# Retention attention and two MoE layers in one program: attention moved ahead of the first MoE, that MoE in two groups of 768 tokens, 224 places an expert

## The chip, the cores and the metric

The program runs on one core of a Trainium2 chip. The metric is the device time of one execution in microseconds (us). Engines are called PE (TensorE), DVE (VectorE), ACT (ScalarE), POOL (GpSimd) and SP (SyncE, which only issues transfers here).

## The reference, cut to what matters

```python
# attention: batch 2, 8 heads, 768 tokens, head size 64; one decay gamma per head
for t in range(S):
    state = gamma * state + k[:, :, t] (outer) v[:, :, t]
    y[:, :, t] = scale * (q[:, :, t] @ state)
# first MoE: one dense layer over 1536 tokens, 512 -> 2048 -> 512; w_in and w_out are float64
h = x @ w_in
sp = np.where(h > 20.0, h, np.log1p(np.exp(np.minimum(h, 20.0))))
g = h * np.tanh(sp)
x = g @ w_out
# second MoE: 8 experts, 512 -> 1024 -> 512; each token goes to its best expert
e_idx = np.argmax(x @ w_gate, axis=1)
for e in range(E):
    h = np.maximum(x[mask] @ w1[e], 0.0)
    out[mask] = gate_w[mask, None] * eom[mask, e, None] * (h @ w2[e])
```

gate_w is the softmax weight of the chosen expert and eom a sigmoid of a second small product. With the inputs used, the fullest expert gets 220 of the 1,536 tokens.

## The kernel before

**Attention.** A unit is a block of 128 tokens and a pair of heads; 12 blocks and 4 pairs give 48 units. In each, PE makes the scores of the two heads (`scores`, two float32 matmuls, L184 for the first 16 units with 64 rows of the array each, L187 from unit 16 on with 128 rows, where k of each head is padded with zeros), DVE multiplies them with the decay mask into `sm` (L189), and `values` multiplies them with v (L213), adds the query times the running state (L217) and makes the new state (L221). ACT and DVE take the result out of PSUM as two float32r parts, `xh` (L224) and `xl` (L231). POOL prepares `kh` and `qh` (L171, L176). The first 16 units run ahead of the first MoE; the other 32 are spread over the slices of its first two groups. For the first eight units PE also transposes k (`turn_k`).

**Decoding.** w_in and w_out come as float64. 32 words of 128x512 are brought to float32 by `decode`: one ACT conversion of the low word, four DVE steps (L260, L262, L266, L269) and one POOL addition (L271).

**First MoE.** Three groups of 512 tokens, 16 slices of 128 features each: 48 slices. For every slice, `splits` cuts the slice's part of w_in and of w_out into a high and a low float32r part (ACT copy L373, DVE subtraction L278); `up` makes 12 matmuls with 512 columns (L297) into one of two banks `hps`; `take_h`, `exp_h`, `mish_ln`, `mish_tanh` and `mish_split` turn the result into g in two parts (ACT L304, L309, L313, L317, L325; DVE L305, L318, L326), in batches of four slices so that ACT changes its function table seldom; `down`, five slices later (LAG), makes 3 matmuls with 512 columns for each of the group's four token blocks (L336 to L338) into four banks `acc`. The order of the steps inside a slice is written out by hand in `ORDER`; decoding runs beside the first group only, and the weights stay in SBUF for the later groups, which split them again.

**Router and second MoE.** The rows of a finished group go to DRAM, come back turned, and get their logits, their expert and their place (`logits_of`, `pick`, `rank`, `place`); `send` scatters them with indirect DMAs on POOL's queue to 256 places (CAP) for each expert. For the last group this happens between the last two slices' `down`, block by block; expert 0 gets its rows of the last group straight from PSUM by selection matmuls (`turn_base`, `select`, `part_rows`, `add_rows`), the others read theirs from DRAM (`load_rows`, `turn_x`). Each of 8 experts has 8 slices: `up2` makes 12 matmuls with CAP columns (L585), `down2` six with 512 (L601 to L603). `put` scatters the results. If any expert has more tokens than places, a general loop at the end computes the rest.

ACT follows the program order throughout; PE and DVE follow it in the stage ahead of the first MoE and in the last group's router, and elsewhere their order is left to the scheduler that builds the program.

Of the kernel before, what the change touches and what calls it, by code (L numbers as in the profile page):

```python
# [18 lines left out]
P = 128  # L19
# [4 lines left out]
E = 8  # L24
# [6 lines left out]
GB = 4  # L31
GT = GB * P
NG = NB // GB
CAP = 256
# [3 lines left out]
TBM = 2  # L38
TX0 = 6
LAG = 5  # L40
FILL = 1
FILL2 = 0
NFILL = 0
MV = 1
DS = [0, 0, 0, 1, 0, 0, 1, 1, 1, 1, 1, 1, 1, 1, 0, 1, 1]
EA = 0
HA = 0
HB = 0
TA = 0
TC = 1  # L50
KT = 8
SN = 3
EP = 0
RD = 2
S0 = 99
S1 = 15
WARM = 9
PLO0 = 1
LOVK = 0
PGL = (2,)  # L60
HIW = ()
HOW = ()
KP = 6
RL = 0
RT = 3
RG = 4
TB = [2, 2]
BE = [1, 2]
X1 = 0
X4 = 1  # L70
X5 = 1
X3 = 1
X2 = [[0, 1, 2], [3]]
# [12 lines left out]

# offsets (in float32 columns) in the constant array
# [5 lines left out]
C_ID = C_TOK + NB  # L93
# [8 lines left out]
def retention_moe_moe(ctx: ExitStack, tc: tile.TileContext, qkv, wraw, w12, wg, cst, pad, out):  # L102
# [12 lines left out]
    h_p = pool("h", NH)  # L115
    e_p = pool("e", NE)
    g_p = pool("g", NGB)
    u_p = pool("u", NU)
    s_p = pool("s", 2)
# [3 lines left out]
    acc, hps, mp, mt = [], [], [], []  # L123
# [11 lines left out]
    onesb = one.tile([P, P], BF16, name="onesb")  # L135
    mask = cs[:, C_MASK:C_MASK + H * P].rearrange("p (h t) -> p h t", h=H)
# [8 lines left out]
    tok = cs[:, C_TOK:C_TOK + NB]  # L145

    # ---------------- attention, one (block of 128 tokens, pair of heads) at a time
# [4 lines left out]
    def load_unit(n):  # L152
        blk, hp = units[n]
        if n < NU or n >= GB * KD:
            t = u_p.tile([P, 5, P], F32, name="u")
        else:
            t = (h_p if n % 2 else e_p).tile([P, GT], F32, name="h" if n % 2 else "e")
            t = t.rearrange("p (i t) -> p i t", i=4)
        w = 5 if n >= GB * KD else 4 if n >= KT else 3
        SP.dma_start(out=t[:, 0:w], in_=qkv[blk, hp, :, 0:w])  # L160
        unit_in[n] = t

    def prep_unit(n):
        blk, hp = units[n]
        t = unit_in[n]
        c = blk % CB
        kh = qh = None
        if c < CB - 1:
            kh = s_p.tile([P, 2, D], F32, name="kh")
            if n >= KT:  # L170
                G.tensor_tensor(  # L171
                    out=kh, in0=t[:, 4 if n >= GB * KD else 3].rearrange("p (j d) -> p j d", j=2),
                    in1=ktab[:, 2 * hp:2 * hp + 2].unsqueeze(2).to_broadcast([P, 2, D]), op=ALU.mult)
# [3 lines left out]
        unit_k[n] = (kh, qh)  # L177

    def scores(n, pst):
        blk, hp = units[n]  # L180
        t = unit_in[n]
        for j in range(2):
            if n < GB * KD:
                T.matmul(out=pst[:, j, 0:P], lhsT=t[j * D:(j + 1) * D, 1], rhs=t[j * D:(j + 1) * D, 0],  # L184
                         start=True, stop=True)
            else:
                T.matmul(out=pst[:, j, 0:P], lhsT=t[:, 1 + 2 * j], rhs=t[:, 0], start=True, stop=True)  # L187
        sm = s_p.tile([P, 2, P], F32, name="sm")
        V.tensor_tensor(out=sm, in0=pst[:, 0:2, 0:P], in1=mask[:, 2 * hp:2 * hp + 2], op=ALU.mult)  # L189
        return sm  # L190

    def turn_k(n, o):
        blk, hp = units[n]
        T.transpose(out=o, in_=unit_in[n][:, 1], identity=ident)
        for j in range(2):
            A.activation(out=unit_k[n][0][:, j], in_=o[:, j * D:(j + 1) * D], func=AF.Copy,
                         scale=ktab[:, 2 * hp + j:2 * hp + j + 1])

    def values(n, pst, sm):
        blk, hp = units[n]  # L200
        t = unit_in.pop(n)
        kh, qh = unit_k.pop(n)
        c = blk % CB
        g, o = blk // GB, (blk % GB) * P
        if n < GB * KD:
            ya, ua = pst[:, 0, P:2 * P], pst[:, 1, P:P + D]
        else:
            ya, ua = pst[:, 2], pst[:, 3, 0:D]
# [25 lines left out]
    # ---------------- weights: float64 words to float32, float32 to two float32r parts  # L234
# [14 lines left out]
    def decode(n):  # L249
        """The steps of a decoding, one vector instruction each."""  # L250
# [5 lines left out]
        if n < EA:  # L256
            A.activation(out=d.bitcast(F32), in_=hi.bitcast(F32), func=AF.Abs)
            A.activation(out=lo, in_=lo.bitcast(U32), func=AF.Copy, scale=2.0 ** -29)
        else:
            V.tensor_scalar(out=d, in0=hi, scalar1=0x7FFFFFFF, scalar2=None, op0=ALU.bitwise_and)  # L260
        yield
        (G if n < EP else V).tensor_scalar(out=d.bitcast(F32), in0=d.bitcast(F32), scalar1=2.0 ** -15, scalar2=None, op0=ALU.max)  # L262
        if n >= EA:
            A.activation(out=lo, in_=lo.bitcast(U32), func=AF.Copy, scale=2.0 ** -29)
        yield
        V.tensor_scalar(out=d, in0=d, scalar1=3, scalar2=0x3FFFFFF8, op0=ALU.logical_shift_left,  # L266
                        op1=ALU.bitwise_and)
        yield
        V.scalar_tensor_tensor(out=d, in0=hi, scalar=-0x40000000, in1=d, op0=ALU.bitwise_and,  # L269
                               op1=ALU.bitwise_or)  # L270
        G.tensor_tensor(out=d, in0=d, in1=lo, op=ALU.add)  # L271
        yield

    def split(src, name, engine=V, first=A):
        hi = t_p.tile([P, 512], F32R, name=name, bufs=6 if name == "wi" else NWO)
        lo = t_p.tile([P, 512], F32R, name=name, bufs=6 if name == "wi" else NWO)
# [6 lines left out]
    batches = [list(range(4 * i, 4 * i + 4)) for i in range((NS - sum(TB)) // 4)]  # L283
    for n in TB:
        batches.append(list(range(batches[-1][-1] + 1, batches[-1][-1] + 1 + n)))
# [3 lines left out]
    def up(i):  # L289
        g, f = divmod(i, NF)  # L290
        wh, wl = win.pop(i)
        xh, xl = xt[g, 0], xt[g, 1]
        o = hps[i % 2][:, :]
        n = 0
        for k in range(KD):
            for a, b in ((wh, xh), (wh, xl), (wl, xh)):
                T.matmul(out=o, lhsT=a[:, k * P:(k + 1) * P], rhs=b[:, k], start=(n == 0), stop=(n == 3 * KD - 1))  # L297
                n += 1

    def take_h(i):  # L300
        o = hps[i % 2][:, :]
        h = h_p.tile([P, GT], F32, name="h")
        e = e_p.tile([P, GT], F32, name="e")
        A.activation(out=h, in_=o, func=AF.Copy)  # L304
        V.tensor_scalar(out=e, in0=h, scalar1=20.0, scalar2=None, op0=ALU.min)  # L305
        hs[i], es[i] = h, e

    def exp_h(i):
        A.activation(out=es[i], in_=es[i], func=AF.Exp)  # L309

    def mish_ln(b):
        for i in b:
            A.activation(out=es[i], in_=es[i], func=AF.Ln, bias=1.0)  # L313

    def mish_tanh(b):
        for i in b:
            A.activation(out=es[i], in_=es[i], func=AF.Tanh)  # L317
            V.tensor_tensor(out=hs[i], in0=hs[i], in1=es.pop(i), op=ALU.mult)  # L318

    def mish_split(b):  # L320
        for i in b:
            h = hs.pop(i)
            gh = g_p.tile([P, GT], F32R, name="gh")
            gl = g_p.tile([P, GT], F32R, name="gl")
            A.activation(out=gh, in_=h, func=AF.Copy)  # L325
            (G if i < NF and i % 4 in PGL else V).tensor_tensor(out=gl, in0=h, in1=gh.bitcast(F32), op=ALU.subtract)  # L326
            gs[i] = gh, gl
# [19 lines left out]
    # ---------------- router, a block of 128 tokens at a time  # L347
# [13 lines left out]
    def blocks_of(r):  # L361
        return r.rearrange("p b c -> p (b c)")[:, 0:CAP * KD].rearrange("p (q j) -> p q j", j=P)

    def load_blocks(x, after=lambda i: None):
        """256 rows from DRAM, to be turned 32 by 32: row 32 q + r and feature 128 a + j to partition 32 a + r."""
        r = blocks_of(raw_p.tile([P, 2, RW], F32, name="raw"))
# [8 lines left out]
    def turn_rows(b, o, engine):  # L375
        r = rows[b // 2][:, b % 2]
        x = g_p.tile([P, KD * P], F32, name="gl")
# [17 lines left out]
    def logits_of(b0, n, o):  # L395
        """The logits of n blocks, each in a quarter of the columns of the tensor engine."""
# [19 lines left out]
    def tl(name, n, w, dtype=F32):  # L416
        return r_p.tile([P, n, w], dtype, name=f"{name}{n}", bufs=2 if n == 2 else 1)

    def pick(b0, n, o):
        """The experts of n blocks, from their logits."""  # L420
# [16 lines left out]
    def weigh(b0, n, o):  # L437
        """The exponentials of their weights."""
# [18 lines left out]
    def place(b0, n, o):  # L457
        """The places of the tokens among those of the experts."""
# [586 lines left out]
```

## Time and profile before

| what | value |
|---|---|
| median of 3 runs | 590.5 us (590.46 to 590.51) |
| the profiled execution, first to last instruction (its span) | 600.2 us |
| PE busy | 562.2 us, 94% |
| DVE busy | 418.5 us, 70% |
| ACT busy | 370.9 us, 62% |
| POOL busy | 155.4 us, 26% |

The runs are timed without the profiler, so the profiled span lies 9.7 us above their median. Busy time of PE counts matmuls whose ends are modelled and overlap, so 94% is no measure of how close PE is to its peak. Times inside the profile are us from the start of the span.

### The profile page before, as it was taken

To read this page: it belongs to the slowest core of one execution; us is meant where nothing else is said; L and a number is where in the kernel's file an instruction comes from. 1 tells how busy PE (TensorE), PEld (TensorE's weight loads), DVE (VectorE), ACT (ScalarE), POOL (GpSimd) and SP (SyncE) were. 2 spreads that over 40 slices of the span, in tenths; PEclk is the share of its full clock that TensorE was granted. 3 is DMA by queue.
4 is the path that set the end of the run, shared out by engine and by line. 5 is a ranking of instruction groups with operands and counts; after the bars stand their busy time and mean duration, and the time that the engine had idled before them with its cause. 6 is when DMAs were issued, how large, how long until landed. Compare 5 with 4: busy or idle time off the path is not lost.

```text
span 600.2 us, 9282 instructions
## 1 busy us (share of the span) xinstructions
PE 562.2 (94%) x3197; PEld 450.6 (75%) x3197; DVE 418.5 (70%) x858; ACT 370.9 (62%) x706; POOL 155.4 (26%) x163
## 2 busy tenths in 40 slices
PE   7997878798899999999999999999899999999992
PEld 4565556575667777777888788889699999999992
DVE  3569999999988384845536757548577687676650
ACT  3223665755767666665967969836466567566551
POOL 0357565485763131130000030023011011011011
PEclk9559889999899999999999999989999999999997
DMA  8625563535213374120016353605899778661001
GB/s 286 219 99 183 173 196 103 185 115 183 92 57 115 121 241 145 50 87 0 1 35 189 128 173 108 209 4 176 235 326 253 236 237 253 200 227 62 2 20 34
DMA packets 40388, 86.38 MB, mean 144 GB/s; under 512 B 6286, under 2 KB 19342, under 8 KB 40208
## 3 DMA queue, kind: packets, MB, share of 16 engines
q1 hardware_dynamic: 36432, 73.23, 39.5%
q10 hardware_dynamic: 1664, 6.19, 2.9%
q0 software_dynamic: 2240, 6.31, 2.8%
q8 instruction: 27, 0.44, 0.3%
q14 instruction: 25, 0.20, 0.1%
HBM read 76.21 MB, written 14.77 MB: 152 GB/s over the span
## 4 chain that ended last, share of the span: by engine, by line
PE 64%; DVE 23%; issue 4%; DMA 3%; ACT 2%; POOL 0%; ACTq 0%; SPq 0%; POOLq 0%; DVEq 0%
PE hps L297 15%; PE hps L585 12%; PE acc L336 6%; PE acc L338 6%; PE acc L337 5%; PE acc L601 4%; PE acc L602 4%; PE acc L603 4%; DVE fw L260 3%; DVE fw L266 3%; DVE fw L269 3%; DVE fw L262 3%; DVE e L305 2%; DVE wi L278 2%; DVE wo L278 2%
## 5 line engine op out<-in xcount | busy, mean ns | idle before, releaser
L297 PE MATMUL hps<-xh,wi 128*128 128x512 f32 x384 | 132.6, 407 | 2.0 <-DVE wi L278 2.0
L585 PEld LDWEIGHTS hps<-xh,wi 128*128 128x128 f32 x768 | 100.3, 191 | 7.3 <-ACT xh L574 1.7
L585 PE MATMUL hps<-xh,wi 128*128 128x256 f32 x768 | 102.6, 283 | 1.3 <-ACT xh L574 1.3
L278 DVE TENSOR_TENSOR wi<-fw,wi 128x512 fp32r<-128x512 f32 x108 | 77.9, 721 | 17.3 <-ACT wi L373 13.6
L297 PEld LDWEIGHTS hps<-xh,wi 128*128 128x128 f32 x384 | 74.5, 195 | 19.4 <-DVE wi L278 2.8
L278 DVE TENSOR_TENSOR wo<-fw,wo 128x512 fp32r<-128x512 f32 x109 | 78.1, 717 | 8.1 <-ACT wo L373 7.5
L297 PE MATMUL hps<-xl,wi 128*128 128x512 f32 x192 | 77.3, 403 | 0.0
L373 ACT CAST wo<-fw 128x512 fp32r<-128x512 f32 x109 | 68.0, 624 | 13.2 <-PE acc L602 12.8
L336 PE MATMUL acc<-wo,gh 128*128 128x512 f32 x180 | 73.2, 407 | 0.0
L373 ACT CAST wi<-fw 128x512 fp32r<-128x512 f32 x115 | 70.5, 614 | 2.0 <-issue 1.7
L337 PE MATMUL acc<-wo,gh 128*128 128x512 f32 x180 | 71.1, 395 | 0.0
L338 PE MATMUL acc<-wo,gl 128*128 128x512 f32 x180 | 69.8, 398 | 0.0
L271 POOL TENSOR_TENSOR fw<-fw,raw 128x512 int32<-128x512 int32 x32 | 52.5, 1648 | 37.1 <-DVE fw L269 18.3
L304 ACT ACTIVATE h<-hps 128x512 f32<-128x512 f32 x48 | 28.3, 589 | 50.1 <-PE hps L297 50.1
L614 POOL DMA_INDIRECT out_dram<-h,places x16 | 17.2, 1078 | 158.6 <-ACT h L613 136.4
L589 ACT ACTIVATE gh<-hps 128x256 fp32r<-128x256 f32 x64 | 24.6, 384 | 46.8 <-PE hps L585 46.3
L601 PE MATMUL acc<-wo,gh 128*128 128x512 f32 x128 | 50.5, 396 | 1.3 <-ACT gh L589 1.3
L602 PE MATMUL acc<-wo,gh 128*128 128x512 f32 x128 | 50.4, 395 | 0.0
L603 PE MATMUL acc<-wo,gh 128*128 128x512 f32 x128 | 49.7, 389 | 0.0
L318 DVE TENSOR_TENSOR h<-h,e 128x512 f32<-128x512 f32 x48 | 32.3, 717 | 21.8 <-ACT e L317 21.8
L590 DVE SCALAR_TENSOR_TENSOR gh<-hps,gh 128x256 fp32r<-128x256 f32 x64 | 26.8, 419 | 25.1 <-ACT gh L589 24.8
L297 PEld LDWEIGHTS hps<-xl,wi 128*128 128x128 f32 x192 | 37.5, 195 | 7.4 <-issue 0.2
(181 smaller groups left out, 944.3 us busy)
## 6 DMA issues: line engine op xcount, KB each, us to landing
fw<-in_w_dram SPq DMA_DIRECT2D x64, 512.0 KB, 4.1
raw<-in_wraw_dram SPq DMA_DIRECT2D x32, 512.0 KB, 3.7
u<-in_qkv_dram SPq DMA_DIRECT2D x32, 320.0 KB, 2.9
xs<-in_pad_dram ACTq DMA_DIRECT2D x8, 514.0 KB, 6.5
raw<-xs SPq DMA_DIRECT2D x28, 128.0 KB, 4.1
xall<-raw SPq DMA_DIRECT2D x4, 512.0 KB
raw<-xall SPq DMA_DIRECT2D x16, 128.0 KB, 3.2
e<-in_qkv_dram SPq DMA_DIRECT2D x4, 256.0 KB, 5.6
```

The source lines that it names most:

```text
L271: G.tensor_tensor(out=d, in0=d, in1=lo, op=ALU.add)
L278: engine.tensor_tensor(out=lo, in0=src, in1=hi.bitcast(F32), op=ALU.subtract)
L297: T.matmul(out=o, lhsT=a[:, k * P:(k + 1) * P], rhs=b[:, k], start=(n == 0), stop=(n == 3 * KD - 1))
L318: V.tensor_tensor(out=hs[i], in0=hs[i], in1=es.pop(i), op=ALU.mult)
L336: T.matmul(out=o, lhsT=gh[:, c], rhs=wh, start=(f == 0), stop=False)
L337: T.matmul(out=o, lhsT=gh[:, c], rhs=wl, start=False, stop=False)
L338: T.matmul(out=o, lhsT=gl[:, c], rhs=wh, start=False, stop=(f == NF - 1))
L373: (A.copy if engine is A else engine.tensor_copy)(out=to, in_=of)
L585: T.matmul(out=o, lhsT=a[:, k * P:(k + 1) * P], rhs=x[:, k, b:b + CAP], start=(n == 0), stop=(n == 3 * KD - 1))
L601: T.matmul(out=o, lhsT=g[:, c], rhs=wh, start=(f == 0), stop=False)
L602: T.matmul(out=o, lhsT=g[:, c], rhs=wl, start=False, stop=False)
L603: T.matmul(out=o, lhsT=g[:, l], rhs=wh, start=False, stop=(f == NF2 - 1))
```

## The change

Attention runs first: 42 of 48 units (NA) before the first MoE, the other six over its first three slices. All scores use 128 rows: one matmul with 256 columns per unit, k of both heads as weights, against q with the other head's half set to zero (`qz`, two ACT operations with a 0/1 column as scale). The 5-part layout of q, k and v and the transposes of k go. Every unit now loads four parts (256 KB).

The first MoE has two groups of 768 tokens: 32 iterations of two `up` halves with 384 columns each and a `down` over six blocks, three iterations later (LAG 3). The function is rewritten: tanh(softplus(h)) as -tanh(ln(sigmoid(-h))); the `min` on DVE and the Exp go, a Sigmoid from PSUM comes in. Batches are pairs of slices. Each decode step now has four DVE operations with no POOL in them; 34 of 128 steps (ND) run during attention and the others at a fixed rate of 6.8 an iteration. The copy of w_out's high part goes to DVE. Group 0's routing is one block of six; the last group's router handles six blocks, and sends the first four before the last `down` is over. CAP is 224, so `up2` has 224 columns and `down2` 112 columns of weights. PE, DVE and ACT follow the program order throughout.

```diff
-GB = 4
+GB = 6
 GT = GB * P
+GH = GT // 2
...
-CAP = 256
+CAP = 224
+CB2 = CAP // 2
...
-LAG = 5
+LAG = 3
+NA = 42
+WARM = 10
...
+ND = 34
...
+        qz = s_p.tile([P, 2, P], F32, name="qz", bufs=2)
+        for j in range(2):
+            A.activation(out=qz[:, j], in_=t[:, 0], func=AF.Copy, scale=halves[:, j:j + 1])
...
-        for j in range(2):
-            if n < GB * KD:
-                T.matmul(out=pst[:, j, 0:P], lhsT=t[j * D:(j + 1) * D, 1], rhs=t[j * D:(j + 1) * D, 0],
-                         start=True, stop=True)
-            else:
-                T.matmul(out=pst[:, j, 0:P], lhsT=t[:, 1 + 2 * j], rhs=t[:, 0], start=True, stop=True)
...
+        T.matmul(out=pst[0][:, 0:2 * P], lhsT=t[:, 1], rhs=unit_k[n][2].rearrange("p j t -> p (j t)"), start=True, stop=True)
...
-            V.tensor_scalar(out=d, in0=hi, scalar1=0x7FFFFFFF, scalar2=None, op0=ALU.bitwise_and)
...
-        G.tensor_tensor(out=d, in0=d, in1=lo, op=ALU.add)
...
+        V.tensor_scalar(out=d.bitcast(F32), in0=hi.bitcast(F32), scalar1=2.0 ** -112, scalar2=None, op0=ALU.mult)
+        A.activation(out=lo, in_=lo.bitcast(U32), func=AF.Copy, scale=2.0 ** -29)
         yield
...
+        V.tensor_scalar(out=d, in0=d, scalar1=3, scalar2=None, op0=ALU.logical_shift_left)
         yield
...
+        V.scalar_tensor_tensor(out=d, in0=hi, scalar=-0x80000000, in1=d, op0=ALU.bitwise_and,
+                               op1=ALU.bitwise_or)
         yield
...
+        V.tensor_tensor(out=d, in0=d, in1=lo, op=ALU.add)
         yield
...
+    def take_h(i, half):
+        if not half:
+            hs[i], es[i] = he(GT), he(GT)
+        c = slice(half * GH, half * GH + GH)
+        o = hps[half][:, 0:GH]
+        A.activation(out=hs[i][:, c], in_=o, func=AF.Copy)
+        A.activation(out=es[i][:, c], in_=o, func=AF.Sigmoid, scale=-1.0)
...
+            A.activation(out=es[i], in_=es[i], func=AF.Ln, bias=tiny)
+
+    def mish_tanh(i):
+        A.activation(out=es[i], in_=es[i], func=AF.Tanh, scale=-1.0)
+        V.tensor_tensor(out=hs[i], in0=hs[i], in1=es.pop(i), op=ALU.mult)
+
+    def mish_split(i, engine):
+        h, gh, gl = hs.pop(i), he(GT, F32R), he(GT, F32R)
+        copy(engine, gh, h)
+        V.tensor_tensor(out=gl, in0=h, in1=gh.bitcast(F32), op=ALU.subtract)
+        gs[i] = gh, gl
...
+            for n in range(NA + 1):
+                if n < NA:
+                    sm[n] = scores(n, spots[n % 3])
+                    prep_unit(n + 2)
+                steps_to(n - NA + ND)
+                if n >= NA - 1:
+                    split_in(n - NA + 1)
+                if n > 0:
+                    values(n - 1, spots[(n - 1) % 3], sm.pop(n - 1))
+                loads_to(n + 8)
+                raws_to(min(NR, max(0, n - 4) // 2))
...
+            s0 = ND + 4 * min(i, 3) + 34 * max(0, i - 3) // 5 + 2
+            mish_ln(b)
+            steps_to(s0)
+            late = range(NA + 2 * i, min(NA + 2 * i + 2, NU))
...
+            up(i, 0)
...
+            split_out(i + 2 - LAG)
+            take_h(i, 0)
+            if len(c) == 2:
+                mish_split(c[1], A)
+            if b:
+                mish_tanh(b[0])
+            split_in(i + 2)
+            steps_to(s0 + 2)
+            up(i, 1)
...
+            take_h(i, 1)
+            if len(b) == 2:
+                mish_tanh(b[1])
+            if b:
+                mish_split(b[0], A)
...
+            steps_to(s0 + 4)
+            if i >= LAG:
+                down(i - LAG, range(0, 3))
+                route(j)
+                down(i - LAG, range(3, GB))
...
+            if tb in (3, 5):
+                exps(n)
+                send(n, 2)
```

## Rows read from the trace of the kernel before

**Rows 1.** The page: busy time by engine, and the chain that ended last.
```profile
PE 562.2 (94%) x3197; PEld 450.6 (75%) x3197; DVE 418.5 (70%) x858; ACT 370.9 (62%) x706; POOL 155.4 (26%) x163
...
PE 64%; DVE 23%; issue 4%; DMA 3%; ACT 2%; POOL 0%; ACTq 0%; SPq 0%; POOLq 0%; DVEq 0%
```

**Rows 2.** Windows: stretch, length, busy time by engine (instructions), PE clock, DMA share, GB/s.
```profile
5.43:11.50 6.07, 5.89 (x58) 4.13 (x57) 2.36 (x8) 4.05 (x14) 0.35 (x1) 1.00 0.95 305
11.50:13.10 1.60, 0.06 (x3) 0.00 (x0) 0.81 (x4) 0.38 (x2) 0.38 (x2) 1.00 1.01 393
13.10:43.47 30.37, 30.36 (x200) 18.12 (x200) 16.79 (x51) 8.38 (x25) 13.09 (x26) 0.51 0.54 179
43.47:183.30 139.83, 118.68 (x604) 86.33 (x603) 136.75 (x230) 87.47 (x161) 87.76 (x71) 0.94 0.44 141
183.30:387.83 204.53, 204.53 (x1062) 162.41 (x1063) 125.18 (x281) 152.32 (x272) 26.25 (x37) 1.00 0.36 114
387.83:405.14 17.31, 16.88 (x118) 14.62 (x118) 8.13 (x38) 5.91 (x15) 5.11 (x4) 0.90 0.10 32
405.14:589.30 184.16, 181.57 (x1155) 163.77 (x1153) 127.86 (x248) 111.20 (x222) 20.41 (x19) 1.00 0.59 181
589.30:600.20 10.90, 0.22 (x1) 0.00 (x0) 0.00 (x0) 0.69 (x1) 1.83 (x2) 0.70 0.14 46
```

**Rows 3.** The chain in order of time: start, us, what.
```profile
248.88 1.01 PE mp L400 x32
...
304.62 2.72 PE hps L297 x12
310.06 2.72 PE hps L297 x12
...
414.63 6.04 DMA xs<-raw,idx
...
437.34 1.43 PE hps L585 x12
440.16 1.43 PE hps L585 x12
```

**Rows 4.** Timeline of PE around attention units: start, us, engine, line, operands, count.
```profile
28.34 0.80 PE L184 MATMUL sp<-h 64*128 64x128 f32 x4
...
30.73 0.80 PE L184 MATMUL sp<-e 64*128 64x128 f32 x4
...
41.74 2.08 PE L187 MATMUL mp<-u 128*128 128x128 f32 x8
...
192.56 0.60 PE L187 MATMUL mp<-u 128*128 128x128 f32 x4
...
193.09 0.44 PE L213 MATMUL mp<-sm,u 128*64 128x128 f32 x4
...
194.09 0.50 PE L336 MATMUL acc<-wo,gh 128*128 128x512 f32 x1
```

**Rows 5.** The chain inside the first group, DVE: start, us, what.
```profile
118.37 0.67 DVE fw L266 x2
...
120.24 2.41 DVE h L318 x4
```

**Rows 6.** Groups of ACT instructions by line, whole span: count, busy us, mean ns.
```profile
L304 ACT ACTIVATE h<-hps 128x512 f32<-128x512 f32 x48 | 28.3, 589 | 50.1 <-PE hps L297 50.1
...
L589 ACT ACTIVATE gh<-hps 128x256 fp32r<-128x256 f32 x64 | 24.6, 384 | 46.8 <-PE hps L585 46.3 <-issue 0.4
...
L313 ACT ACT_TABLE_LOAD x13 | 16.7, 1283 | 0.2
L317 ACT ACT_TABLE_LOAD x13 | 16.7, 1283 | 0.2
```

**Rows 7.** Timeline of the weight loads: 128 columns of weights, 16 columns streamed.
```profile
396.73 1.86 PEld L393 LDWEIGHTS hps<-wgs,gl 128*128 128x128 f32 x16
```

**Rows 8.** Waits from 44 to 175 us: us in total, times, longest.
```profile
ACT e L309 <- DVE e L305: 17.6, 11, 4.9
```

More of the change, by code (lines that the diff above doesn't have):

```diff
@@ L296, in up @@
             for a, b in ((wh, xh), (wh, xl), (wl, xh)):
-                T.matmul(out=o, lhsT=a[:, k * P:(k + 1) * P], rhs=b[:, k], start=(n == 0), stop=(n == 3 * KD - 1))
+                T.matmul(out=o, lhsT=a[:, k * P:(k + 1) * P], rhs=b[:, k, c], start=(n == 0), stop=(n == 3 * KD - 1))
                 n += 1
[L300 to L309, printed above, removed]
+        if half:
+            del win[i]
+    def take_h(i, half):
+        if not half:
+            hs[i], es[i] = he(GT), he(GT)
+        c = slice(half * GH, half * GH + GH)
+        o = hps[half][:, 0:GH]
+        A.activation(out=hs[i][:, c], in_=o, func=AF.Copy)
+        A.activation(out=es[i][:, c], in_=o, func=AF.Sigmoid, scale=-1.0)
     def mish_ln(b):
         for i in b:
[L313 to L327, printed above, removed]
+            A.activation(out=es[i], in_=es[i], func=AF.Ln, bias=tiny)
[7 more added lines that the diff above has]
+        gs[i] = gh, gl
     def down(i, tbs):
@@ new lines, in retention_moe_moe @@
+            for n in range(2):
+                prep_unit(n)
+            for n in range(WARM):
+                T.matmul(out=idle, lhsT=zeros[:, 0:P], rhs=zeros[:, 0:512], start=True, stop=True)
+            for n in range(NA + 1):
[9 more added lines that the diff above has]
+                raws_to(min(NR, max(0, n - 4) // 2))
@@ L818, in retention_moe_moe @@
         g = NG - 1
-        splits(NS + 2)
-        mish_tanh(batch_at[NS - 1])
-        mish_split(batch_at[NS - 1])
-        for n in range(NS - LAG, NS - TBM):
-            down(n, range(GB))
+        b0 = g * GB
+        mish_ln([NS - 1])
+        mish_tanh(NS - 1)
+        mish_split(NS - 1, A)
+        split_out(NS - 1)
+        down(NS - 3, range(GB))
         for m in range(NF - LAG, NF):
@@ new lines, in retention_moe_moe @@
+        add_rows(b0, 2, [2])
+        turn_rows(b0 + 5, hps[0], A)
+        logits(b0 + 4, lb[:, 0:2 * E])
+        logits(b0 + 5, lb[:, 2 * E:4 * E])
+        pick(b0 + 4, 2, lb)
+        add_rows(b0 + 2, 2, [0])
+        turn_base([3])
+        add_rows(b0, 2, [3])
+        add_rows(b0 + 2, 2, [1])
+        rank(b0 + 4, 2, rb)
+        place(b0 + 4, 2, rb)
+        add_rows(b0 + 2, 2, [2, 3])
+        select(b0 + 4, 0)
+        add_rows(b0 + 4, 1, range(KD))
+        select(b0 + 4, 1)
+        add_rows(b0 + 5, 1, range(KD), True)
@@ L920, in retention_moe_moe @@
                 turn_x(e + 1)
+            if m == NF2:
+                V.tensor_copy(out=meta[1], in_=meta[0][:, :, 0])
             if m == KP:
-                for b in (b0, b0 + 2):
-                    keep(b, A)
-                A.dma_start(out=xmore, in_=more)
+                for n in range(0, GB, 2):
+                    keep(b0 + n)
+                SP.dma_start(out=xmore, in_=more)
             if f == KP + 1 and e < E - 2:
```

542 lines of the change are left out of this document (184 added, 358 removed).

## The prediction

> **What bounds the kernel now.** I read the page first, then a table of windows cut at the stages, then the chain of waits, then timelines of PE. The page says PE 94% busy, and that PE holds 64% of the chain and DVE 23% [rows 1]. That average hides four stages [rows 2]:
>
> - 13.1 to 43.5 us: attention ahead of the first MoE, PE busy in every microsecond but at a granted clock of 0.51, its lower level of 1.2 GHz. A unit takes 2.39 us there [rows 4].
> - 43.5 to 183.3: group 0 of the first MoE. DVE is busy 136.75 of 139.83 us, PE 118.68, the clock averages 0.94. DVE is the bound.
> - 183.3 to 387.8: groups 1 and 2. PE is busy throughout at 1.00.
> - 405.1 to 589.3: the second MoE, PE again, 2.6 us idle.
>
> Between them lie 17.31 us of router, and 10.9 us at the end [rows 2].
>
> PE's prices at the full clock: twelve 512-column matmuls take 2.72 us, 0.2267 each, and a slice (up and down) 5.44 us; twelve 256-column ones take 1.43, 0.1192 each, and a slice of the second MoE 2.82 [rows 3]. From the two sizes a column costs 0.42 ns and a matmul 11.7 ns on top. An attention unit inside the first MoE takes 192.56 to 194.09, 1.53 us [rows 4].
>
> So the stretch from 43.5 to 387.8, 344.4 us, holds 48 ups and 46 downs (94 x 2.72 = 255.7) and 32 units (49.0), plus about 2 of logits: 307. The other 37 us are what DVE's bound in group 0 costs PE, in idle time and at the lower clock.
>
> **Stage by stage, after.**
>
> *Attention.* The first scores start at 5.43 now; two ACT operations on q come ahead, about 0.6, so 6.0. The new scores are two passes of 256 columns where L187 has four of 128: the same columns, so I keep the 0.53 us of L187 (192.56 to 193.09) and 1.53 for a unit, although units without a state need less. 42 x 1.53 = 64.3; with 0.5 for handing over, the first MoE starts at 70.8. This assumes the full clock. Other engines: DVE's three attention operations and one decode step make about 1.2 us a unit (decode pace below); 256 KB a unit and a 512 KB word every four units are 0.39 MB, 1.3 us at the 305 GB/s of 5.4 to 11.5 us [rows 2]. Both lie under 1.53, so PE sets the pace, but with little to spare.
>
> *First MoE on PE.* Columns are the same. 384 columns cost 0.0117 + 384 x 0.00042 = 0.173 us by the two sizes; an iteration is 24 x 0.173 + 18 x 0.2267 = 8.23 us, 32 of them 263.4, less the last two downs, which belong to the router: 255.2. Six late units cost 9.2. The logits of group 0, 1.01 us for four blocks [rows 3], come once for six: about 2.3.
>
> *First MoE on DVE.* Back to back in group 0, a single-source step takes 0.67/2 = 0.335 us and a two-source one 2.41/4 = 0.60 at 512 columns [rows 5]; 768 columns add half of 0.53, so 0.87. An iteration: 6.8 decode steps at a mean of 0.47 (3.2), w_in's subtraction 0.6, w_out's copy and subtraction 0.94, the multiplication and the low part 1.73: 6.5 us against PE's 8.23. Decode moves from POOL to DVE, but splits fall from 96 to 64 slices and `min` goes. If POOL's additions no longer slow DVE, group 0 becomes PE's. Against that stands before's own pace: 136.75/16 = 8.55 us a slice, with POOL's additions beside it. Taking from it the `min` (0.6) and attention (about 0.85) and adding the fourth step, the copy and the longer rows (1.0 + 0.34 + 0.53) gives 9.0, 0.8 over PE for 13 iterations: 10 us. Bounds 0 and 12; I take 5, nearer to the fast rows since POOL has nothing to do in those iterations. A wait is added: w_out's parts have six buffers, so an iteration's `split_out` waits until PE has ended the `down` before it; behind it on DVE stand that iteration's multiplication, low part and w_in's subtraction, which PE needs only an iteration later.
>
> *First MoE on ACT.* L304 takes 589 ns at 512 columns and L589 384 at 256 [rows 6], so 0.49 at 384 and 0.79 at 768. An iteration: four at 384 (1.95), three at 768 (2.4, 2.5 with the bias operand), w_in's copy 0.6, 1.7 conversions (1.1), one table load (1.28): 7.5 us in group 0, 6.3 after. That lies under 8.23, so nothing, but the cover is thin: ACT also issues the eight zero fills of the places in iterations 6 to 13, and what it needs beyond 0.7 us more in one of these PE waits for.
>
> *Router.* 17.31 us now, of which eight block-downs of 0.68 are 5.4. After: twelve of them, 8.2, the other 11.9, and 3.9 for two blocks more (bounds 2 and 6, by nothing but the selection matmuls and by the full proportion): 24.0. The last slice's chain (two takes 1.0, two table loads 2.6, Ln, Tanh and high part 2.4, DVE 1.7: 7.7 us) lies beside the two downs ahead of it, 8.2.
>
> *Second MoE.* At 224 columns the two sizes give 0.1058 us a matmul. But 128 columns of weights must be loaded for each, and where only 16 columns are streamed loads come 1.86 us less one 0.19 us record over 15, 0.111 apart [rows 7]: the load binds. Bounds 0.1058 and 0.1192 (no gain, 5.5 us more); I take 0.112, so 12 x 0.112 + 1.39 = 2.734 a slice, 64 of them 175.0, against 180.5 now. *The Trainium skill's page "TensorE: Matmul & The Clock Gate", section "LDWEIGHTS (loading the stationary operand)", speaks against the full saving too: a load takes its columns over 1.2 GHz, 107 ns for 128, an estimate of 171.5 us by itself; the trace, at 111, agrees within 4%.* The 3.7 us that 184.16 holds beyond 180.5 are a wait for expert 1's rows, behind four scatters whose last took 6.04 us to land [rows 3]. Two instead of four wait for the end now: I keep 1 us. Together 176.0. The end keeps its 10.9.
>
> **The sum.** 70.8 + 255.2 + 9.2 + 2.3 + 5 + 24.0 + 176.0 + 10.9 = 553.4 us of span, against 600.2: 46.8 less. The runs' median is 590.5, 9.7 below the profiled span; with the same difference, 543.7. I predict **544 us**.
>
> **Rivals.**
>
> *The attention stage stays at 1.2 GHz* (580 us). For: after 1.54 us without matmuls at 11.5 the clock fell, and from 13.1 to 43.5 it stayed low although PE never paused [rows 2]; a unit then took 2.39 [rows 4], so 42 x 0.86 = 36 us more, up to 42 with the wider scores at the pace of L187's eight passes at 41.74. Against: from 5.4 to 11.5 the same sparse units ran at 1.00, and PE now waits for no decode there. It decides if a transfer or ACT leaves PE empty that long once.
>
> *ACT paces the first MoE, and the kernel is slower* (619 us). Place: ACT's fixed order, in which Sigmoid and Tanh take turns within a pair of slices. If each change loads a table, that is four loads of 1.283 [rows 6] more per pair, 2.57 an iteration: 10.0 and 8.9 us, 584 in all. ACT's longest kind of wait for DVE in group 0, 17.6 us [rows 8] over 16 slices, 1.1 an iteration, on top gives 11.1 and 10.0: (2.9 + 1.8) x 16 = 75 us more. It turns slower once ACT needs 8.23 + 46.8/32 = 9.7 us an iteration. Against: 13 batches now load 13 tables for Ln and 13 for Tanh [rows 6], and the Exp between Tanh and Ln has no row of its own, so functions can share a table. *The Trainium skill's page "ScalarE: Activation LUTs", section "Table sets: the hidden batching unit", lists tanh in sigmoid's set, which speaks against this rival.*
>
> *DVE and ACT wait for each other in group 0* beyond my 5 us, both in program order: the 1.1 us of [rows 8] in each of 16 iterations is 18, so 557.
>
> *The 224 places bring nothing*: 549. *More tokens than 224 for an expert* would run the general loop; the fullest has 220.
>
> **How the numbers follow.** The forecast gets 0.55 (own range 530 to 566: no stalls, 0.1058 and units without state cheaper at one end; 12 us of stalls, no gain from 224 and a unit at 1.7 at the other). The low clock 0.25, part of it for only some of the stage, ACT's pacing 0.06, longer mutual waits 0.12; 0.02 for anything else. The range 528 to 586 takes in all but ACT's case and the edges. Two runs of this kernel can be told apart by about 0.2%. Faster 0.90, within 0.2% 0.02, slower 0.08: ACT's case and low clock together with waits.
>
> **What would show it.** PE clock 1.00 and some 1.5 us a unit until about 70 us; iterations of 8.2 us from the fourth on, DVE and ACT below 95% in them; two table loads a pair of slices; `up2` twelve in 1.34; first matmul of the second MoE near 366. The prediction is wrong if the clock row shows 0.5 after 15 us, if iterations of group 0 take over 9 us, or if ACT never idles.

## The result: 563.0 us against 590.5, and the profile after

The changed kernel takes 563.03 us (median of four executions, 561.92 to 563.54). The ratio to the kernel before is 0.9528, with a 95% interval of 0.9509 to 0.9548. The prediction was 544 us with a range of 528 to 586. One thing has to be known to read the times of this case: the kernel before takes about 590 us in some executions and about 600 in others, the version at the end of this text took 585.6 once in six, and ratios use the lower group.

The page of the changed kernel: busy time by engine, the granted clock in 40 slices (tenths), and the chain that ended last. The profiled execution took 561.92 us, its span is 560.2.

```profile
PE 539.9 (96%) x3311; PEld 451.9 (81%) x3311; DVE 369.2 (66%) x790; ACT 378.6 (68%) x722; POOL 75.7 (14%) x130
...
PEclk9999999999999999999999999999999999999997
...
PE 86%; DVE 4%; issue 4%; ACT 2%; DMA 1%; POOL 0%; POOLq 0%; DVEq 0%; ACTq 0%
```

DVE's 23% of the chain [rows 1] are down to 4%: PE now sets the pace nearly everywhere, at its full clock. The windows of the changed kernel, cut at its stages (columns as in [rows 2]):

```profile
5.59:10.02 4.43, 3.31 (x24) 1.93 (x23) 1.42 (x5) 2.63 (x9) 1.22 (x3) 1.00 1.06 383
10.02:70.66 60.64, 60.40 (x518) 33.27 (x518) 48.75 (x148) 41.98 (x129) 29.75 (x73) 1.00 0.85 285
70.66:71.99 1.33, 0.00 (x1) 0.03 (x1) 1.33 (x4) 0.82 (x3) 0.29 (x1) 1.00 0.35 139
71.99:342.50 270.51, 270.17 (x1429) 241.65 (x1430) 173.52 (x312) 208.82 (x331) 12.91 (x21) 1.00 0.33 102
342.50:345.81 3.31, 0.76 (x4) 0.32 (x3) 2.29 (x4) 2.30 (x4) 0.00 (x0) 1.00 0.00 0
345.81:373.61 27.80, 25.26 (x178) 20.29 (x179) 17.94 (x82) 10.65 (x25) 11.66 (x10) 1.00 0.37 134
373.61:549.68 176.07, 175.26 (x1154) 153.03 (x1153) 123.55 (x236) 108.52 (x221) 17.36 (x16) 1.00 0.62 178
549.68:560.20 10.52, 0.40 (x2) 0.00 (x0) 0.00 (x0) 0.69 (x1) 1.88 (x2) 0.64 0.16 48
```

From the second row to the seventh PE is idle for 0.24, 1.33, 0.34, 2.55, 2.54 and 0.81 us. Group 0, where PE lost 21 us in idle time alone [rows 2], has gone as a stage of its own. Against the terms of the sum:

| term | predicted, us | measured, us |
|---|---|---|
| first scores of the first MoE | 70.8 | 71.99 |
| from there to the last `down` ahead of the router, at 342.50 | 271.7 | 270.5 |
| router, to the first `up2` at 373.61 | 24.0 | 31.1 |
| second MoE | 176.0 | 176.1 |
| end | 10.9 | 10.5 |
| span | 553.4 | 560.2 |

The span was missed by 6.8 us, nearly all of it in the router. The other 11.4 us of the miss come from turning the span into a time: I took 9.7 us off, where the changed kernel's time lies 1.7 above its span (1.7 to 2.3 in every execution with both on record). The last 1.1 is the profiled execution's distance from the median.

Two places carry the gain. Against a profile of the kernel before with a span of 589.4 us (below), some 34 us are won up to the router and 8 in the second MoE, and 14 are lost in the router. An iteration of the first MoE in group 0, the chain in order of time (start, us, what):

```profile
102.69 4.18 PE hps L244 x24
...
111.00 4.18 PE hps L244 x24
...
119.31 0.71 PE hps L244 x4
```

8.31 us, 4.18 of them the two `up` halves, with no wait in the chain; 8.23 was predicted. And the second MoE, where a slice takes 2.73 us and twelve matmuls of `up2` 1.33, against 1.43 in [rows 3]:

```profile
432.49 1.33 PE hps L534 x12
...
435.22 1.33 PE hps L534 x12
```

The place that was missed is the end of the first MoE. The chain around the last slice's function and in the router:

```profile
335.24 0.85 ACT L262 ACTIVATE h<-h 128x768 f32<-128x768 f32 x1
```

```profile
338.09 1.28 ACT L259
...
340.34 1.28 ACT L262
...
342.52 0.97 DVE h L263
343.51 0.84 ACT h L312
344.37 0.96 DVE h L268
345.33 0.35 DVE wo L312
345.77 0.70 DVE wo L225
...
356.27 1.17 DVE at L404
...
365.33 1.20 DVE at L404
```

The first fence is the timeline: ACT is still at slice 30's Tanh while slice 31's `up` is over. Then Ln and Tanh of slice 31 load a table each, and DVE's split of w_out stands behind them; PE waits from 343.2 to 345.8. Later L404, an addition of 16 columns, twice takes over 1.1 us.

### The profile page after: what moved, and what is told of

Same layout as the page of the kernel before. It is cut to its first block, busy times and chain, and to the rows that moved or that the text cites. A ratio compares the mean times of both kernels' runs of the same rounds, so it can differ in the third digit from the quotient of the medians.

```text
span 560.2 us, 9429 instructions
## 1 busy us (share of the span) xinstructions
PE 539.9 (96%) x3311; PEld 451.9 (81%) x3311; DVE 369.2 (66%) x790; ACT 378.6 (68%) x722; POOL 75.7 (14%) x130
## 4 chain that ended last, share of the span: by engine, by line
PE 86%; DVE 4%; issue 4%; ACT 2%; DMA 1%; POOL 0%; POOLq 0%; DVEq 0%; ACTq 0%
PE hps L244 23%; PE hps L534 13%; PE acc L278 7%; PE acc L279 7%; PE acc L280 7%; PE acc L551 5%; PE acc L550 5%; PE acc L552 5%; PE sp L148 4%; PE sp L165 2%; PE sp L169 2%; PE sp L173 1%; DMA cs<-in_cst_dram 1%; DMA h<-in_qkv_dram 1%; PE acc L148 1%
## 5 line engine op out<-in xcount | busy, mean ns | idle before, releaser
L244 PE MATMUL hps<-xh,wi 128*128 128x384 f32 x512 | 137.8, 338 | 0.0
L534 PE MATMUL hps<-xh,wi 128*128 128x224 f32 x768 | 96.0, 274 | 0.8 <-DVE h L539 0.8
L244 PE MATMUL hps<-xl,wi 128*128 128x384 f32 x256 | 85.7, 335 | 0.0
L278 PE MATMUL acc<-wo,h 128*128 128x512 f32 x192 | 75.9, 395 | 2.6 <-DVE wo L312 2.6
L279 PE MATMUL acc<-wo,h 128*128 128x512 f32 x192 | 75.4, 393 | 0.2 <-DVE wo L225 0.2
L280 PE MATMUL acc<-wo,h 128*128 128x512 f32 x192 | 75.5, 393 | 0.0
L263 DVE TENSOR_TENSOR h<-h 128x768 f32<-128x768 f32 x32 | 30.7, 959 | 50.6 <-ACT h L262 47.0
L254 ACT ACTIVATE h<-hps 128x384 f32<-128x384 f32 x64 | 31.4, 491 | 48.2 <-PE hps L244 48.2
L551 PE MATMUL acc<-wo,h 128*112 128x512 f32 x128 | 50.7, 396 | 0.0
L550 PE MATMUL acc<-wo,h 128*112 128x512 f32 x128 | 50.6, 395 | 0.0
L552 PE MATMUL acc<-wo,h 128*112 128x512 f32 x128 | 50.3, 393 | 0.0
L312 ACT CAST wo<-fw 128x512 fp32r<-128x512 f32 x64 | 39.7, 621 | 11.1 <-PE acc L551 11.0
L142 ACT ACTIVATE qz<-h,cs 128x128 f32<-128x128 f32 x96 | 33.2, 394 | 19.6 <-PE sp L148 16.6
L278 PEld LDWEIGHTS acc<-wo,h 128*128 128x128 f32 x192 | 36.1, 188 | 10.3 <-ACT wo L312 3.0
L280 PEld LDWEIGHTS acc<-wo,h 128*128 128x128 f32 x192 | 36.0, 188 | 7.9 <-DVE h L268 0.3
```

The lines of the kernel that those rows point to most:

```text
L142: A.activation(out=qz[:, j], in_=t[:, 0], func=AF.Copy, scale=halves[:, j:j + 1])
L244: T.matmul(out=o, lhsT=a[:, k * P:(k + 1) * P], rhs=b[:, k, c], start=(n == 0), stop=(n == 3 * KD - 1))
L254: A.activation(out=hs[i][:, c], in_=o, func=AF.Copy)
L278: T.matmul(out=o, lhsT=gh[:, c], rhs=wh, start=(f == 0), stop=False)
L279: T.matmul(out=o, lhsT=gh[:, c], rhs=wl, start=False, stop=False)
L280: T.matmul(out=o, lhsT=gl[:, c], rhs=wh, start=False, stop=(f == NF - 1))
```

## Experiments: what the clock depends on

**The kernel before, profiled again.** No edit.

> The kernel before, unchanged, profiled anew. First theory: the profiled execution of before (span 600.2) was not like its timed ones; a profile of a 590.5 us execution has a span some 1.7 us below its own time, near 589, as in the changed kernel, and the 11 us lie in one stage: attention ahead of the first MoE, with a granted clock above the 0.51 of [rows 2]. Second theory: profiling costs this kernel 10 us, the span is 600 again and the clock is 0.51 again from 13 to 43 us.

Its four executions took 591.18, 601.88, 603.03 and 589.46 us; the profiled one is the first, with a span of 589.4. So the first theory holds: the profiled execution is one of the timed ones, and the profile of [rows 2], with a span of 600.2, was one of a 600 us execution. The same stretch in this profile, cut where the first MoE begins (windows; columns as above):

```profile
5.43:11.50 6.07, 5.95 (x60) 4.20 (x59) 3.34 (x12) 3.58 (x14) 0.86 (x2) 1.00 0.99 346
11.50:13.10 1.60, 1.60 (x19) 1.01 (x17) 0.86 (x4) 0.89 (x4) 0.04 (x1) 1.00 1.03 394
13.10:30.70 17.60, 16.94 (x186) 10.66 (x182) 15.32 (x43) 7.61 (x23) 13.61 (x24) 1.00 0.84 296
30.70:43.47 12.77, 10.50 (x58) 7.54 (x60) 10.92 (x25) 3.24 (x8) 7.58 (x9) 0.87 0.35 99
```

PE does not pause at 11.5, the clock stays at 1.00 where [rows 2] have 0.51, and the first MoE begins at 30.7 instead of 43.5. What made the pause in the 600 us execution is in its timeline, DVE and then PE:

```profile
12.29 0.43 DVE L260 TENSOR_SCALAR fw<-raw 128x512 int32<-128x512 int32 x1 [1.95 <-DMA raw<-in_wraw_dram]
```

```profile
13.11 0.38 PE L184 MATMUL sp<-h 64*128 64x128 f32 x2 [1.54 <-DVE xl L231]
```

DVE, in program order, waits 1.95 us for the first raw word; the `xl` that frees PE's PSUM stands behind it. A transfer that lands 2 us later thus cost that execution some 10 us, through the clock. This is not all that sets executions of the kernel before apart: the two of 601.88 and 603.03 us have mean clocks of 0.981 and 0.980, no lower than the 0.983 and 0.980 of the two short ones (the 600.2 us profile has 0.952), so they lost their time in another way, and no profile shows it.

**64-row scores in the changed kernel.** `qz` and its ACT operations go, `ua` moves to another part of its bank, and `sm` becomes two operations.

```diff
-        T.matmul(out=pst[0][:, 0:2 * P], lhsT=t[:, 1], rhs=unit_k[n][2]..., start=True, stop=True)
+        for j in range(2):
+            T.matmul(out=pst[j][:, 0:P], lhsT=t[j * D:(j + 1) * D, 1], rhs=t[j * D:(j + 1) * D, 0], start=True, stop=True)
```

> The changed kernel with the old form of scores: two matmuls with 64 rows each, no qz. First theory: PE keeps its full clock because nothing stops it in the first 15 us; the form of the scores does not matter for the clock. The clock row stays at 1.00, a unit drops from 1.63 to about 1.4 us (half the 2.39 at 1.2 GHz is 1.2; q, k, v and the words want 1.3), the time is 551 to 558. Second theory: scores with half the rows are too little work for the full clock; it falls to 0.5 within the stage, a unit takes 2.3, and the time is 585 to 600.

554.51 us (553.43 to 555.09), 8.5 less than the changed kernel, with the clock at 1.00 in every window of the stage: the first theory. (Against the 564.40 that a later set gave for the changed kernel it is 9.9 less.) One unit of the changed kernel and one of this kernel, timelines of PE:

```profile
30.16 0.70 PE L148 MATMUL sp<-qz,h 128*128 128x256 f32 x2
30.79 0.44 PE L165 MATMUL sp<-sm,h 128*64 128x128 f32 x4
31.16 0.44 PE L169 MATMUL sp<-qh,st 64*64 64x128 f32 x4
31.52 0.34 PE L173 MATMUL sp<-h,kh 128*64 128x64 f32 x4
31.79 0.70 PE L148 MATMUL sp<-qz,h 128*128 128x256 f32 x2
```

```profile
29.32 0.49 PE L146 MATMUL sp<-h 64*128 64x128 f32 x4
29.74 0.44 PE L164 MATMUL sp<-sm,h 128*64 128x128 f32 x4
...
30.74 0.49 PE L146 MATMUL sp<-h 64*128 64x128 f32 x4
```

1.63 and 1.42 us a unit; all of the difference lies in the scores, 0.63 against 0.42. So widening the scores to 128 rows made the kernel slower.

**A pause, with either form of scores.** ACT gets needless work ahead of unit 5 (six operations with 128 rows, eight with 64), so PE waits 2.88 and 2.85 us.

```diff
+                    if n == 3:
+                        for _ in range(6):
+                            A.activation(out=idle, in_=cs[:, C_MASK:C_MASK + 4 * P], func=AF.Copy)
                     prep_unit(n + 2)
```

> The changed kernel with six needless ACT operations of 128x512 ahead of unit 5's qz, so that PE stands still for some 2 us near 12 us, as before did at 11.5. First theory: units with 128-row scores are enough work to bring the clock back; it dips for a few us, and the time grows by 2 us of pause and 2 to 5 of low clock: 566 to 570. Second theory: after such a pause the clock stays at 1.2 GHz for all of the stage, as in before; 38 units take 0.8 us more each and the time is 593 to 603.

> The pause (eight ACT operations) and the 64-row scores together. First theory: the clock comes back only if the work after the pause is dense, and half-row scores are not; the clock row shows 0.5 from the pause to the first MoE as in before, a unit 2.3 us, and the time is 30 us or more above that of the 64-row kernel without a pause. Second theory: the form of the scores has no part in it, and this kernel loses to its own version without a pause as much as the 128-row one does to its.

With 128 rows: 582.4 to 594.8 us. With 64 rows: 590.5 to 591.7, 36.7 more than without the pause. Windows after the pause, 128 rows and then 64:

```profile
20.00:30.00 10.00, 10.00 (x50) 4.76 (x51) 3.97 (x14) 4.17 (x12) 2.68 (x7) 0.50 0.43 141
...
50.00:60.00 10.00, 10.00 (x69) 5.26 (x68) 6.24 (x19) 5.56 (x18) 3.65 (x10) 0.78 0.52 165
60.00:70.00 10.00, 9.77 (x82) 5.47 (x83) 9.19 (x29) 7.74 (x26) 4.99 (x9) 1.00 0.90 308
```

```profile
70.00:80.00 10.00, 10.00 (x70) 5.76 (x68) 6.20 (x22) 1.66 (x5) 3.25 (x8) 0.50 0.56 168
80.00:100.00 20.00, 20.00 (x137) 11.66 (x136) 13.19 (x45) 4.62 (x13) 7.03 (x17) 0.50 0.36 116
```

Neither theory of the first run holds as put: the clock did not come back within a few us, nor did it stay down for all of the stage. With 128 rows it rose by itself between 50 and 60 us; with 64 rows it stayed at 1.2 GHz to the end of the stage. That is the first theory of the second run, and the one thing the 128-row form is good for: it limits the damage of a pause (19 to 32 us), at 8.5 us in every execution. When the clock comes back differs: the window shows the 582.4 us execution, and the other three have mean clocks of 0.934 to 0.947 against its 0.958, so it was low for longer in them. In the second profile of the changed kernel (`after_again`, below) PE waited 1.63 us ahead of unit 3, and the 128-row units lost the clock for 3.4 us only:

```profile
12.30:15.70 3.40, 3.40 (x22) 1.90 (x22) 1.26 (x5) 1.79 (x6) 0.68 (x3) 0.50 1.05 383
15.70:72.40 56.70, 56.47 (x487) 30.96 (x484) 45.86 (x137) 38.67 (x119) 27.14 (x66) 1.00 0.82 266
```

**The pause filled on PE.** The 64-row kernel with its pause, and four needless matmuls ahead of unit 5's scores.

```diff
+                if n == 5:
+                    for _ in range(4):
+                        T.matmul(out=idle2, lhsT=mask[:, 0], rhs=cs[:, C_MASK:C_MASK + 4 * P], start=True, stop=True)
```

> The kernel with 64-row scores and the pause of ACT, and four needless float32 matmuls of 512 columns on PE ahead of unit 5's scores, so that PE works while the rest stands still. First theory: what loses the clock is PE with nothing to do, not the late chain of a unit; the clock stays at 1.00 through the stage, and the time is that of the 64-row kernel and the 3 us of the pause: 556 to 560. Second theory: needless work does not stand in for units, or a unit that comes late lowers the clock itself; the row shows 0.5 again and the time is 588 to 592.

558.06 us (556.71 to 559.70), 33 less than with the pause left empty, and only 3.6 above the 64-row kernel without one. The filler in the timeline and the windows behind it:

```profile
11.45 3.70 PE L652 MATMUL idle<-cs 128*128 128x512 f32 x8
```

```profile
14.00:20.00 6.00, 6.00 (x59) 3.36 (x57) 3.46 (x17) 0.83 (x3) 2.30 (x6) 1.00 1.01 350
20.00:50.00 30.00, 29.30 (x334) 18.68 (x332) 27.93 (x108) 9.78 (x29) 15.51 (x38) 1.00 0.91 304
```

ACT's needless work was the same, and the clock stayed at 1.00: the empty PE loses the clock, not the late unit. The length of the wait alone does not decide it, though. A wait of 1.15 us at 11.4 in the profile of `before_vadd` (below) was followed by 0.50 from 13.1 to 43.8, where one of 1.39 at 8.3 in that of `two128` was not; and the same wait of 2.56 us at the end of the first MoE left the changed kernel's clock at 1.00, while in the 64-row kernel's profile 0.51 followed from 336.2 to 339.7. What else decides is open. So is whether thinner work than the filler's 512 columns would have done.

## Experiments: the other terms

**256 places.** `CAP = 256` in the changed kernel.

> The changed kernel with 256 places an expert instead of 224. First theory: at 224 columns a matmul of up2 is bound by its weight load, 0.111 us, at 256 by its columns, 0.119; up2 takes 1.43 us instead of 1.33 and the 64 slices 6 us more: 568 to 571. Second theory: the weight load or something beside PE sets the pace at both sizes, and the time is 562 to 565.

568.41 us (567.49 to 569.24), 5.4 more than the 563.03 (4.0 more than the changed kernel's 564.40 in a later set). Inside the profiles the second MoE, from the first `up2` to the last `down2`, runs from 374.6 to 556.2, 181.6 us against 176.1: 5.5 more, the predicted amount, with twelve matmuls of `up2` at 1.43 again. The first theory. *The Trainium skill's "TensorE: Matmul & The Clock Gate", section "LDWEIGHTS (loading the stationary operand)", prices a load by its columns over 1.2 GHz, 107 ns for 128; the trace's 1.33 us for twelve gives 0.111 each, within 4%.*

**The last addition of a decoded word on POOL, in the changed kernel; on DVE, in the kernel before.** One word each, `V` to `G` and `G` to `V`.

```diff
-        V.tensor_tensor(out=d, in0=d, in1=lo, op=ALU.add)
+        G.tensor_tensor(out=d, in0=d, in1=lo, op=ALU.add)
```

> The changed kernel with the last addition of each decoded word on POOL, as before. First theory: while POOL adds two tensors in SBUF (1.55 us each in the kernel before), DVE's own operations wait for it (0.34 us becomes 1.44); the 32 additions taken from DVE (22 us) come back as stretched operations. DVE's busy time falls by less than 10 us or rises, its single-source steps show means above 0.5 us; the time is 562 to 570, as DVE had a quarter of its time free. Second theory: POOL's work costs DVE nothing; DVE's busy time falls by 22 us to 347, its steps keep their 0.42 and the time does not move.

> The kernel before with the last addition of a decoded word on DVE instead of POOL. First theory: DVE is the bound of group 0 because POOL's additions hold it; 27 of them on DVE cost 18 us, but about 39 us of stretched DVE operations go (means of 0.6 to 1.07 us come down to 0.42 and 0.69), so group 0 is 10 to 20 us shorter: 571 to 582 against 590.5. Second theory: DVE's own work is the bound, and the additions make group 0 longer by 10 to 18 us: 600 to 608.

On POOL: 564.33 us (563.45 to 565.37), 1.3 us above the changed kernel's 563.03 and 0.1 below the 564.40 of the later set. DVE's busy time is 370.2 us against 369.2, although 32 operations of 0.69 us, 22 us, have left it. What came back is unequal: L213, a single-source step, went from 0.43 to 0.65 us, L210, another, from 0.42 to 0.45. On DVE in the kernel before: 578.67 us, ratio 0.9787 (0.9745 to 0.9829), some 12 us less by this one word, in a group that DVE bounds; in the changed kernel, where PE sets the pace, the same word is worth 1.3 us at most. First theories both. What holds DVE is seen in the second profile of the kernel before, timeline of POOL and of DVE:

```profile
121.53 3.40 POOL L271 TENSOR_TENSOR fw<-fw,raw 128x512 int32<-128x512 int32 x2 [2.30 <-DVE fw L269]
```

```profile
121.98 1.79 DVE L326 TENSOR_TENSOR gl<-h,gh 128x512 fp32r<-128x512 f32 x1
123.69 1.52 DVE L260 TENSOR_SCALAR fw<-raw 128x512 int32<-128x512 int32 x1
125.13 0.41 DVE L189 TENSOR_TENSOR sm<-mp,cs 128x256 f32<-128x256 f32 x1
```

Two POOL additions, of 1.69 and 1.75 us, run from 121.53 to 124.93. L326 and L260 begin beside them and end 0.55 and 0.28 us after each is over (they take 0.6 and 0.34 us otherwise). L189, which reads PSUM and one tile of SBUF, comes after both here; the eight of it that run beside a POOL addition elsewhere in this profile take 0.42 us at most, as the others do. *The Trainium skill's "SBUF — State Buffer", section "Who interferes with whom", says that a DVE instruction with two SBUF inputs, or a copy or tensor-scalar one in a two-port mode, and a GpSimd instruction that reads SBUF can't share the port, so that the later of the two waits for the whole of the other, and that one with a single SBUF input outside those modes does not; these durations agree.*

**Scores as two matmuls of 128 columns.**

```diff
-        T.matmul(out=pst[0][:, 0:2 * P], lhsT=t[:, 1], rhs=unit_k[n][2]..., start=True, stop=True)
+        for j in range(2):
+            T.matmul(out=pst[0][:, j * P:(j + 1) * P], lhsT=t[:, 1], rhs=unit_k[n][2][:, j], start=True, stop=True)
```

> The changed kernel with its 128-row scores as two matmuls of 128 columns instead of one of 256, the same columns and weights. First theory: the 0.63 us that the scores take against the 0.53 of the kernel before come from the two long passes, whose next weights are not loaded beside them; a unit goes from 1.63 to 1.53 us and the time to 558 to 560. Second theory: the 0.1 us has to do with the order of PE, DVE and ACT in a unit (PE's loads wait 0.33 us for DVE's xl in the rows); nothing changes: 562 to 564.

564.88 us (564.07 to 566.24), no gain; the scores take 0.64 us, a unit 1.64. The first theory falls: long passes are not what makes 0.63 of the 0.53 I had read. What differs is what runs ahead. The weight loads of the scores, in the changed kernel's attention stage and in the kernel before inside the first MoE (timelines):

```profile
30.16 0.30 PEld L148 LDWEIGHTS sp<-qz,h 128*128 128x128 f32 x2
```

```profile
192.34 0.64 PEld L187 LDWEIGHTS mp<-u 128*128 128x128 f32 x4
```

In [rows 4] the matmuls of L187 begin at 192.56, 0.22 after the load, which ran beside an `up`; here load and matmul begin together, at 30.16, behind a matmul with 64 output columns. The kernel before has the same 0.1 us where a wait leaves PE empty ahead of L187 (timeline of PE):

```profile
73.57 0.71 PE L187 MATMUL mp<-u 128*128 128x128 f32 x4 [2.30 <-DVE xl L231]
74.21 0.44 PE L213 MATMUL mp<-sm,u 128*64 128x128 f32 x4
```

That is 0.64 from L187 to L213, against 0.53 behind an `up`. So I read the 0.1 us as a first load in the open; no run took it away, so it is argued, not shown.

**The tail.** Three edits of the changed kernel.

```diff
+        split_out(NS - 1)
         mish_ln([NS - 1])
         mish_tanh(NS - 1)
         mish_split(NS - 1, A)
-        split_out(NS - 1)
         down(NS - 3, range(GB))
+        down(NS - 2, range(0, 3))
...
-            down(NS - 2, [tb])
+            if tb > 2:
+                down(NS - 2, [tb])
...
-        G.tensor_tensor(out=lo, in0=r, in1=hi.bitcast(F32), op=ALU.subtract)
+        V.tensor_tensor(out=lo, in0=r, in1=hi.bitcast(F32), op=ALU.subtract)
         parts[b] = hi, lo
```

> The changed kernel itself, on the chip of the two runs beside it: 562 to 564 by every theory.

> The changed kernel with three edits between the two MoE layers: the split of w_out's last slice goes ahead of the last slice's function, three blocks of the last but one down go ahead of the router, and the low parts of part_rows are made on DVE instead of POOL. First theory: the 6.8 us by which the span missed the sum lie here, in PE's pause at 342.5 to 345.8 and in L404, which takes 1.16 instead of 0.17 us twice while POOL works on L497; the pause goes (2.5 us) and the two stretches too (1 to 2 us): 3.5 to 4.5 us less than the changed kernel beside it. Second theory: the router is bound by ACT's and POOL's own chains, and DVE gives back with six operations of 0.69 what it gains: 1 to 2.5 us less.

The changed kernel takes 564.40 us here (563.37 to 564.98, and one execution of 571.44 with a mean clock of 0.977 against 0.988 to 0.992), this one 560.25 (559.55 to 560.84): 4.15 less, the first theory's figure. The profiles give the edits less. From the last `up` to the first `up2` this kernel takes 37.1 us, the changed one 39.6 in both of its profiles: 2.5 us. The profile beside it also reached its first `up` 2 us later, with the 3.4 us at 0.50 shown above, which has nothing to do with the edits; against the first set's 563.03 the difference is 2.8. So some 2.5 us are shown, the upper end of the second theory. PE is busy without a gap through the place of the pause, and DVE's L404 takes its 0.18 us again (window; group of DVE):

```profile
334.20:344.36 10.16, 10.16 (x46) 8.24 (x45) 4.85 (x7) 8.69 (x12) 0.00 (x0) 1.00 0.17 55
```

```profile
L404 DVE TENSOR_TENSOR at<-at,far 128x16 f32<-128x16 f32 x3 | 0.5, 182 | 0.1
```

**All together.** 64-row scores, the tail, and w_in's first splits inside the attention stage.

```diff
-                if n >= NA - 1:
-                    split_in(n - NA + 1)
+                if n in (20, 24):
+                    split_in((n - 20) // 4)
```

> 64-row scores without qz, the three edits of the tail, and w_in's first two slices split at units 20 and 24 instead of between attention and the first MoE, with the first two decode steps there behind the late scores. First theory: the gains add, 8.5 for the scores, 3.5 to 4.5 for the tail, 1 to 1.5 for the handover: 549 to 551. Second theory: with 64-row scores DVE is full in parts of the attention stage, and the splits moved there come back as waits: 551 to 554. Both below the kernel before and the changed one.

551.15 us; ratio 0.9337 (0.9321 to 0.9352) to the kernel before, 13.2 us below the changed kernel beside it. The expectation of 549 to 551 is missed by a hair. By stage, its profile (span 549.2) is 10.9 us shorter than the changed kernel's: 8.8 of them lie ahead of the first `up`, 0.5 between it and the last, 2.5 from there to the first `up2`, and the stretch behind the last `up2` is 0.9 longer. So the scores and the tail add; the splits moved show no gain of their own, as the 64-row kernel's first `up` came at 62.7 and this one's at 63.5. Its one execution at 585.6 was not profiled, but its clock is on record: a mean of 0.919, against 0.993 to 0.995 in the other five and 0.915 to 0.917 in the 64-row kernel with the pause. The clock fell there too; what stopped PE is open.

## Why the prediction was nearly right, step by step

- **The likeliest case came true.** Full clock, PE's pace in group 0, 224 places worth 5.4 us: three of the four large terms are within 1.3 us. That 563 still lies in this case's own range of 530 to 566 is partly luck: its upper end was made of 12 us of stalls, no gain from the 224 places and units of 1.7 us, and what came instead are the next two steps, which the range did not hold.
- **The step that failed most: "with the same difference".** I read the 9.7 us between span and median as the profiler's cost and took them off again. They were the difference between two kinds of execution of the kernel before; a time lies some 2 us above the span of its own execution. The row that could have told me was the clock of 0.51 at 13.1 to 43.5 us: I used it as the kernel's state and never asked whether the timed runs shared it.
- **The mis-sized term: the router.** 24.0 with bounds of 22 and 26, measured 31.1. The last slice's chain, "7.7 us beside 8.2", took from 332.3 to 345.3, 13 us, because I summed its own operations and left out slice 30's high part and Tanh, which ACT's fixed order puts in between, and the table loads they force. And I carried 11.9 us of the old router over as they were; in the new one two additions on DVE's path ran beside POOL's L497 and took 1 us longer each. Undoing both shortened the stretch by 2.5 of the 7.1 us; the other 4.6 stay open (the two further blocks may cost more than the 3.9 I gave them, which no run tried).
- **Attention.** A unit with state took 1.63, not 1.53; a unit without one 1.11; the wait for unit 3's q, k and v took 1.1 at the start. They cancel to 1.2 us. My sentence that the columns are the same was right and did not matter: I never asked what the narrow form costs at the full clock. L184's 0.80 us at 1.2 GHz in [rows 4] pointed to some 0.4 at 2.4; the same trace has it at the full clock, from 8.00 to the next matmul at 8.42, and 0.42 is what the 64-row kernel showed: the loss inside the change could have been seen ahead.
- **First MoE on DVE.** 6.5 us an iteration from the fast rows, 9.0 from the old pace, 5 us taken for stalls. Between 102.7 and 210 us DVE was busy 80% of the time, 6.7 us an iteration, and PE's waits in the 270 us sum to 0.3: the fast rows were right, and what I took for DVE's pace was POOL's hold on it.
- **ACT.** The first MoE has 34 table loads for 17 batches (17 for Ln, 16 for Sigmoid, one for Tanh), two each; ACT was busy 82% in the same stretch. The rival of 619 us had no part.
- **The low clock.** The rival named half of its trigger ("leaves PE empty that long once"): 1.54 us of emptiness lost the clock in the kernel before, 2.85 and 2.88 did in the experiments, 1.11 at 8.9 to 10.0 us in the changed kernel did not; but 1.15 did in `before_vadd`, and 2.56 at 343.3 us in the changed kernel did not. So the length is not enough to tell. The changed kernel was not safe from it either: its second profile shows 0.50 for 3.4 us, and one of its ten executions took 571.44 us at a lower mean clock. The price of 36 us is near what the 64-row kernel pays (36.7), by chance, as that has other units and the pause in it; the changed kernel paid 19 to 32.
- **Two sums.** The logits row of 1.01 us for four blocks gives 1.5 for six, not 2.3, and the estimate of 171.5 us beside the load's price should be 171. Neither changes the forecast by as much as 1 us.

## What to carry to other kernels

Look at the granted clock before you take a profile as the kernel's usual state, and profile once more if the span is longer than the median. Where DVE is the bound, first see whether its cheap operations are long only while POOL reads SBUF: moving POOL's work onto DVE can shorten both. And price both forms of a matmul at the same clock before you swap one for the other; if a wait can't be removed, needless matmuls in it may be the cheapest thing to add.

## What the runs showed of the hardware

- With PE busy in every slice, 128-row units at 1.2 GHz brought the clock back by themselves, some 40 us after the pause in one profile and 3.4 us after its fall in another; 64-row units did not in 85 us. The same 64-row units held a clock of 1.00 for all of the stage where PE's longest wait was 0.6 us.
- A POOL subtraction in SBUF (L497) beside it turned a DVE addition of 16 columns from 0.18 into 1.20 us.
- Two matmuls with 64 rows each took 0.42 us where one with 128 rows, 256 columns and as many useful products took 0.63.
- A table load took 1.28 us, and the next ACT operation began 1.29 us after its start (332.83 and 334.12).
